# One output transfer of 128 partitions in place of four of 32

## The chip, the cores and the metric

The kernel runs on one core of one Trainium2 chip, as one program in one launch. The metric is the device time of that program in microseconds (us). The kernel before has a median of 546.88 us over three runs (542.97 to 548.76).

## What is computed

Two independent heads work on 2048 positions of width 576, and their results stand side by side in an output of 2048 rows of 1152 float32. The left half is a long convolution; the right half is a linear attention with learned feature maps.

```
# left half: the convolution
K = 2.0 * einsum("dn,dnl->dl", C, exp((A * dt)[:, :, None] * pos)).real
y = irfft(rfft(u^T, 2L) * rfft(K, 2L), 2L)[..., :L]
a = y^T + u * D_skip
# right half: linear attention, 32 heads of width 18
q, k, v = split(x @ wqkv)
phi(z) = concat([softmax(z @ w_phi), softmax(-(z @ w_phi))])
o = phi(q) (phi(k)^T v) / (phi(q) (phi(k)^T 1) + 1e-6)
b = o @ wo
out = concat([a, b], axis=-1)
```

## The kernel before, in words

The convolution is done by a Fourier transform in two factors, written as matrix products. Its inverse has two stages. `product` (L890) multiplies the spectra of the input and of the convolution's kernel for an eighth of the frequencies, does the first inverse factor, and stores the two halves of its result to scratch in DRAM (`zd`, L956). `last` (L963) does the second inverse factor. It runs 16 times: for each of two halves of the 576 columns, and in each half for eight groups of four residues `cb` to `cb + 3`. One call loads a tile `zi` of 128 rows by 4 x 288 numbers (L966, 576 KB; in the second half three of every four calls put it in a buffer named `cs`), does eight small matmuls that fill four bands of 32 PSUM partitions (one band for each residue, recorded at the helper line L295), copies the 128 x 576 result to an SBUF tile `ot` on ScalarE or VectorE (L300), and stores it (L979).

Where the tile goes sets the form of that store. Band `n` belongs to residue `n + cb`. Its 32 partitions hold 32 blocks, with two rows of 288 numbers each, so in DRAM a band is 64 pieces of 1152 bytes, 32 output rows apart. The kernel before stores each band with a transfer of its own: 32 partitions in SBUF, 64 pieces in DRAM, 72 KB.

All transfers are issued by SyncE (SP) on one queue, in an order that is written out by hand: `ORDER` is a list of operation numbers for the whole program, and each engine runs its own operations in that order, waiting in place for what the next one needs. The other operations that the prediction speaks of:

- `query_tile` of the attention ends with a matmul into PSUM, a copy into a buffer `ot`, and a store of 128 rows of 2304 bytes (L589, 288 KB). `ot` is one pool of three buffers; `last`, `query_tile` and a short step in the parameters share it, so a fourth copy waits until the store of the first has landed.
- `product` loads `ub` (L904, two transfers of 128 x 2 x 288 for each spectrum) and the matrix `ff` (L895, 256 KB).
- The transfers with narrow outer dimensions are the folds of the attention weights (L357, 126 or 72 rows), the attention state on its way through DRAM (L508 and L526 with 126 rows, L523 with 18 rows of 7 pieces) and the skip weights (L863, four pieces).

Every transfer also waits for the landing of the one eight places before it in the queue, since eight semaphores are used in turn.

Of the kernel before, what the change touches and what calls it, by code (L numbers as in the profile page):

```python
# [27 lines left out]
HD = D // 2  # L28
# [140 lines left out]
class Plan:  # L169
# [34 lines left out]
    def op(self, eng, cost, fn, r=(), w=(), with_=(), table=None, busy=1.0, lock=False, mode=(128, 128), add=None):  # L204
        deps = set()
        for b in r:
            deps.update(b.writers)
        for b in w:
            deps.update(b.readers)
        k = len(self.ops)  # L210
        eng, alt = eng if isinstance(eng, tuple) else (eng, None)
        cost, alt = cost if alt is None else cost[0], alt and (alt, cost[1])
        for b in r:
            b.readers.append(k)
        for b in w:
            b.writers.append(k)
        bufs = list({id(b): b for b in (getattr(x, "home", x) for x in (*r, *w, *with_)) if not isinstance(b, Mark)}.values())
        fill = [b for b in w if b.tag == "ps" and b.writers == [k] and not b.readers] if eng == "pe" else []
        fill = [add] if add else fill
        self.ops.append([eng, cost, fn, deps, bufs, 0.0, table, busy, lock and eng, (self.unit, 0.0, self.part), mode, fill[0] if fill else None, alt, add])  # L220
# [47 lines left out]
def c_dma(nbytes, run=4096):  # L268
    return nbytes / run * (0.35 + 0.0029 * run)
# [7 lines left out]
def body(tc, nc, i, out, ctx):  # L277
    pl = Plan()
    pe, dve, act, pool, sp = nc.tensor, nc.vector, nc.scalar, nc.gpsimd, nc.sync
# [12 lines left out]
    B, op = pl.buf, pl.op  # L292

    def mm(o, l, r, start=True, stop=True, skip=False):
        pe.matmul(o, l, r, start=start, stop=stop, skip_group_check=skip)  # L295

    def copy(eng, dst, src, r, w, n, with_=(), **kw):

        if eng == "any":
            op(("act", "dve"), (c_act(n), c_dve(n)), lambda e: act.activation(dst(), src(), AF.Copy) if e == "act" else dve.tensor_copy(  # L300
                dst(), src()), r=r, w=w, with_=with_)
        elif eng == "act":
            op("act", c_act(n), lambda: act.activation(dst(), src(), AF.Copy, **kw), r=r, w=w)
        else:
            op("dve", c_dve(n), lambda: dve.tensor_copy(dst(), src()), r=r, w=w)
# [657 lines left out]
    def last(cb, half):  # L963
        pl.at("last", 8 * half + cb // 4)
        yo, zi = B("ot", [128, 2, HD]), B("cs" if half and cb % 8 else "zi", [128, 4, HD])
        op("sp", c_dma(128 * 4608), lambda: sp.dma_start(  # L966
            zi.t, zd[half].t.rearrange("q (r b) d -> (q r) b d", r=2)[:, cb:cb + 4]), r=[zd[half]], w=[zi])
        ps = B("ps", [128, 2, HD], banks=2)
        pl.step("l1")

        def f():
            for n in range(4):
                for r in range(2):
                    mm(ps.t[32 * n:32 * n + 32, r], w3.t[64 * r:64 * r + 64], zi.t[64 * r:64 * r + 64, n])
        op("pe", 480, f, r=[zi, w3], w=[ps], mode=(64, 32))
        copy("any", lambda: yo.t, lambda: ps.t, [ps], [yo], D)
        for n in range(4):
            st = out.ap[0][0]
            op("sp", c_dma(32 * 2304, 1152), lambda n=n: sp.dma_start(bass.AP(  # L979
                tensor=out.tensor, offset=out.offset + (n + cb) * st + HD * half, ap=[[64 * st, 32], [32 * st, 2], [1, HD]]),  # L980
                yo.t[32 * n:32 * n + 32]), r=[yo])

    for half in range(2):
        for cb in range(0, 32, 4):
            last(cb, half)
# [68 lines left out]
1901 1939 1904@52 659 1900 1938 2087 770 1902@3 2038 1924 1927 1934 1937 687@57 807 771 1940@6 1925 1928 2039 772 705 660 808 1903 688 809 706 707 810  # L1054
2040@02 1930 1929 689 1941x 2200 690 691 1931@4 1932 1980 1993@64:3 2041 773x 2042 1995x 1994 1981@20 1989@64 1982x 2044 1983x 2043 774@2 708 1996 775
1990 733 709 710 711x 776 734 735 736 777 1984 778 779 1991 692@0 1985@62 1987 812@4 811 714@2 2045 715 1986x 1992 813 712@3 1988 844 713x 716@6 780
2368 2180 693 717 781 718@7 721@6 782 814 738@2 2369@4 719 694 722 720 783 784 2179 2175@0 881 2370 845 846 847 723 2183@6 2181@4 737 2389 2176 724@01
815 816 2182 725 2184 726 727 739 2185 728 817 882 883x 849@4 848 785x 850 2207 661 730@6 786@0 787 851 2372 2201 695 884 2202 2373 2250 2186 852 729
790@1 731 2187 788@0 818 819 820 2208 2375 2189 2188 2374 789 2203@4 2371 791x 732 2205@6 2390@0 2204 2243 2206 2211@4 740 2209@2 2212 2391 2190@60
2191 792@4 795@5 2307 2210 2192 821 2244 2193x 822x 823@2:6 2194 2196 2195 2242 2213x 793 2197 796 2249 2214x 2247@0 824 797 794 853 2245@6 2376@2  # L1060
2248 2246 2253@0 2347 2377 2251@4 2215@62 2198 2199 2254 2252 741 2327 885@0 2216 798@23 742 2328 799 2217 2218x 825@4 827@5 2326 800 801 826x 886
2329@6 2334 2333 828x 802 2392 2219 887 2330 2394 2382 2331@4 2332 743 2335@2 2337@6 2220 888 2336 2256 2255 2257@04 889 2258 2285 832@2 744 890 2338
2286 2259 829@3 803@4 2339x 745 2284 833 830 834 2383@6 2393 891 831 2384 2289@0 2287@2 2260 2291 892 746 2290x 835@67 893 836 894 837 2288 804 747
838 839 2261 2395 2340 2341@02 2292 2293@6 805 2295@4 748 2262 2342 2361 753@2 751@3 2343 2306 2313 2294 2296 752 754x 841@0 2305 749@3 2308@6 750
2310@4 2309x 2312 2316@2 2311 2344 2314@6 2317 2345 2381 2265 2378 755@4 2298 2297 758@5 2315 756 759 757 760 895 896x 2346 2299@26 2380 918 919 920x
761@45 762 840 806 921 2379 2270 763 2264 899@4 2300 764 2319 2348@6 2301 2318 842 2263 2266@2 900x 2267 2268@0 765 2271 2223 2388 2272@4 2349x 2303
2302x 2354 2274@6 2304 2269 955 854 2273 855 2386 856 922@2 857 2320@04 2275 923 2385 2321 2276x 901@4 897@5 956 957x 766@6 958x 898 858 767 902 2387
2229 843 2322 2222 2350 2221 2323 2228 2277 924 2362@4 2226@0 2324 2352 925 926 2224@2 2363x 2232@4 2325 2396 768 2227 927 2225 2233 2351 859 2278@60
2279 2353 2280 769 2230@2 864@4 906@5 2281 2364 2367 2355@0 2365 2366 2397@6 2282 2231 2356 2398 2234x 2283 2235x 2359 2357 2358 903@2 904 907 2236@06
905 862@3 908 909@25 865x 2237 860@4 2238 959@6 2399 960 2360 863 2239x 861x 928 866@3 910 869@4 929 930 931 911 912 2240 913 932 961 962 933 914@0  # L1070
934@2 935 938@5 2241 963 2402 870 2401 2400 939 867 964 965 966 871 868 936@6 915 916 2445 2452 937x 2446@2 2447 2417 2453@4 967 2454x 2438 943@7 917
968 969 872@60 2418@2 2431 940@1 873 874 2448 2456 2457 2449 875 876 941 944 970 971@6 975@0 878@4 972 945 2419 942 946@17 2458 947 973@6 2451 2450
877 879 976x 974x 948 2410 2455 2420 2422 2421 2423 2432@2 2439@0 2440 949 2403 2411@4 880 980@6 981 982 2424 950 2433 977@0 2444 951@2 978 2441 2436
979 983@10 2412 2442 984 2443 985 2437 986 2404@6 2435 2415 2434 2405x 2425@4 2426 2414 952 2416 2413 2409 2408 2407 2406 2428 2430 953 954 2427 2429
987 988@6 989 990 991
"""


# [16 lines left out]
```

## Time and profile before

| what | value |
|---|---|
| median of three runs | 546.88 us (542.97 to 548.76) |
| the profiled execution's own time | 545.11 us |
| its span, first to last instruction | 543.3 us |
| granted TensorE clock | 0.998 |
| TensorE busy | 521.5 us (96% of the span) |
| VectorE, ScalarE, GpSimd busy | 455.9, 382.1, 328.8 us |
| DMA engines, mean busy share of the SP queue's packets | 61.5% |
| stores of `last` (L979) | 64 issues of 72 KB, first at 421.3 us, last at 539.4 us |

Times inside the profile count from the span's start. An issue of a transfer is shown on `SPq`, with the time that SP needed for it; the data moves later, in packets on the core's 16 DMA engines. "DMA share" is the mean busy share over these 16 engines. Of the packets the page tells how many are under 512 bytes, under 2 KB and under 8 KB. "PE busy" is modelled and counts pipelined matmuls to their end.

### The profile page before, as it was taken

The numbers are of one execution on the slowest core, as the hardware profiler recorded it, in microseconds if no ns is written. First come the engines' busy times: TensorE is split into PE (matmuls) and PEld (weight loads), VectorE is DVE, ScalarE is ACT, GpSimd is POOL, SyncE is SP. The second block draws the span as 40 slices with busy tenths as digits, with TensorE's granted clock in tenths as the row PEclk, the third lists the DMA queues.
The fourth block names the chain that finished last, engine by engine and source line by source line (L and its number), as shares of the span: only waits on it lengthen the run. The fifth ranks groups of instructions, "written<-read, shape, count | busy, mean of one in ns | idle before, by whom it ended". The sixth has DMA issues, their size and how long they took to land.

```text
span 543.3 us, 19242 instructions
## 1 busy us (share of the span) xinstructions
PE 521.5 (96%) x8192; PEld 435.9 (80%) x8192; DVE 455.9 (84%) x716; ACT 382.1 (70%) x555; POOL 328.8 (61%) x456
## 2 busy tenths in 40 slices
PE   8999999999999989999999999999899999999995
PEld 7999899888888767888878666766689877776984
DVE  7999899898868889999989996999974889787641
ACT  4868798798559799889689977989733444343332
POOL 1173885958777775982758998997433617434300
PEclk9999999999999999999999999999999999999999
DMA  8936711244245678246664588756458789998785
GB/s 235 326 105 195 281 45 31 101 139 134 89 139 190 207 241 294 83 128 196 229 205 118 153 265 250 241 180 194 131 173 271 234 281 293 287 281 260 265 252 157
DMA packets 86163, 107.01 MB, mean 197 GB/s; under 512 B 5698, under 2 KB 70338, under 8 KB 86078
## 3 DMA queue, kind: packets, MB, share of 16 engines
q1 hardware_dynamic: 86078, 105.79, 61.5%
q8 instruction: 64, 1.05, 0.8%
q14 instruction: 21, 0.17, 0.1%
HBM read 61.22 MB, written 44.54 MB: 195 GB/s over the span
## 4 chain that ended last, share of the span: by engine, by line
PE 69%; DVE 13%; DMA 7%; ACT 4%; issue 3%; SPq 2%; POOL 1%; DVEq 0%; ACTq 0%; POOLq 0%
PE psum L295 63%; PE psum L549 3%; DMA ff<-in_ff_dram 2%; DMA dram<-zi 2%; PE psum L237 2%; DVE ac L314 1%; DVE cs L816 1%; SPq L979 1%; PE psum L577 1%; DMA cs<-dram 1%; DVE e L310 1%; DMA ub<-dram 1%; DVE e L314 1%; DVE small L434 1%; DVE small L437 1%
## 5 line engine op out<-in xcount | busy, mean ns | idle before, releaser
L295 PE MATMUL psum<-vh,x 128*128 128x288 f32 x576 | 123.6, 301 | 0.5 <-ACT ks L300 0.5
L295 PE MATMUL psum<-wh,x 128*128 128x288 f32 x576 | 124.1, 302 | 0.0
L757 POOL TENSOR_TENSOR cs<-cs,pi 128x32 int32<-128x32 int32 (+4 forms) x180 | 108.5, 608 | 8.0
L295 PEld LDWEIGHTS psum<-wh,x 128*128 128x128 f32 x576 | 94.1, 188 | 7.7 <-issue 4.2
L295 PEld LDWEIGHTS psum<-vh,x 128*128 128x128 f32 x576 | 94.0, 188 | 5.4 <-issue 3.2
L295 PE MATMUL psum<-vl,x 128*128 128x288 f32 x320 | 93.8, 295 | 0.0
L295 PE MATMUL psum<-wl,x 128*128 128x288 f32 x320 | 93.7, 295 | 0.0
L811 ACT ACTIVATE psum<-psum 128x512 f32<-128x512 f32 x108 | 59.9, 588 | 15.4 <-PE psum L295 14.9
L295 PEld LDWEIGHTS psum<-vl,x 128*128 128x128 f32 x320 | 60.2, 188 | 0.0
L295 PEld LDWEIGHTS psum<-wl,x 128*128 128x128 f32 x320 | 60.2, 188 | 0.0
L310 POOL TENSOR_TENSOR x<-zo,x 64x128 fp32r<-64x128 f32 (+1 forms) x30 | 25.4, 848 | 46.3 <-ACT x L394 35.1
L310 POOL TENSOR_TENSOR e<-e,small 128x1152 f32<-128x1152 f32 (+1 forms) x24 | 41.2, 1720 | 14.5 <-DVE small L450 7.8
L815 DVE TENSOR_TENSOR cs<-psum,cs 128x1024 f32<-128x1024 f32 x36 | 43.6, 1212 | 3.7 <-ACT psum L811 3.6
L310 POOL TENSOR_TENSOR e<-small,e 128x576 f32<-128x576 f32 x26 | 30.6, 1177 | 25.4 <-DVE small L437 23.6
L816 DVE TENSOR_TENSOR cs<-psum,cs 128x1024 f32<-128x1024 f32 x36 | 43.6, 1214 | 1.4 <-PE psum L295 1.3
L295 PE MATMUL psum<-ub,ff 64*32 64x288 f32 x1024 | 40.0, 410 | 4.3 <-DMA ff<-in_ff_dram 1.9
L295 PEld LDWEIGHTS psum<-kvb,fT 126*128 126x128 f32 (+1 forms) x320 | 38.3, 188 | 7.2 <-issue 2.9
L295 PEld LDWEIGHTS psum<-cs 128*32 128x32 f32 x2304 | 34.1, 110 | 11.2 <-issue 2.9
L295 PE MATMUL psum<-cs 128*32 128x64 f32 x2304 | 40.0, 220 | 2.6 <-DVE cs L816 0.9
L295 PE MATMUL psum<-kvb,fT 126*128 126x133 f32 (+1 forms) x320 | 41.6, 280 | 0.1
L440 ACT ACTIVATE e<-e 128x1152 f32<-128x1152 f32 x32 | 37.0, 1164 | 2.7 <-POOL e L310 1.3
L781 ACT ACTIVATE cs<-cs 128x1040 f32<-128x1040 int32 x36 | 38.3, 1064 | 0.6 <-POOL cs L776 0.4
(156 smaller groups left out, 1115.2 us busy)
## 6 DMA issues: line engine op xcount, KB each, us to landing
dram<-zi SPq DMA_DIRECT2D x32, 576.0 KB
ub<-dram SPq DMA_DIRECT2D x64, 288.0 KB
dram<-zo SPq DMA_DIRECT2D x32, 288.0 KB
zo<-in_xT_dram SPq DMA_DIRECT2D x24, 320.0 KB
zi<-dram SPq DMA_DIRECT2D x12, 576.0 KB
ub<-in_u_dram SPq DMA_DIRECT2D x16, 288.0 KB
xd<-x SPq DMA_DIRECT2D x8, 576.0 KB
x<-xd SPq DMA_DIRECT2D x8, 576.0 KB
```

The lines of the kernel that those rows point to most:

```text
L237: self.matmul(t[0:cols, 0:n], self.zero.t[0:rows, 0:cols], self.data.t[0:rows].bitcast(BF16)[:, 0:n], start=not o[13], stop=not o[13], ski ...
L295: pe.matmul(o, l, r, start=start, stop=stop, skip_group_check=skip)
L310: op(eng, [c_dve(n[0]) if e == "dve" else c_pool(n[1]) for e in eng], lambda e: (dve if e == "dve" else pool).tensor_tensor(dst(), a(), b( ...
L314: op(eng, c_dve(n) if eng == "dve" else c_pool(n), lambda: e.tensor_tensor(dst(), a(), b(), op=alu), r=r, w=w, with_=with_, lock=eng == "p ...
L434: op("dve", c_dve(D), lambda: dve.tensor_reduce(two(top.t), v(), axis=AX.X, op=ALU.max, negate=True), r=[p], w=[top])
L440: op("act", c_act(1152) + 40, lambda: act.activation(e.t, e.t, AF.Exp), r=[e], w=[e], table="exp")
L549: pe.transpose(tp.t[0:m, j - j0, :], e.t[:, sign, 7 * g:7 * g + GRP[g], :].rearrange("p h f -> p (h f)"), ident.t)
L757: op("pool", c_pool(2 * n * W), lambda n=n, j=j: pool.tensor_tensor(x()[:, :, :, n:2 * n], x()[:, :, :, 0:n], pi.t[:, j:j + 2, gs].bitcast ...
L781: act.activation(cs.t[:, 1], cs.t[:, 1].bitcast(I32), AF.Sin, scale=TURN)
L811: op("act", c_act(512), lambda b=b: act.activation(b.t, b.t, AF.Exp), r=[b], w=[b], table="exp")
L815: op("dve", c_dve(64 * W), lambda: dve.tensor_tensor(F(), both(M.t), F(), op=ALU.mult), r=[M, cs], w=[cs])
L816: op("dve", c_dve(64 * W), lambda: dve.tensor_tensor(E.t[:, :, :, 32:64], both(up.t), cs.t[:, :, :, 0:32], op=ALU.mult), r=[up, cs], w=[E])
```

## The change

The loop over the four bands in `last` goes. One transfer takes the whole tile of 128 partitions, and the DRAM side has one more dimension, outermost, for the four residues. The hand-written order is renumbered; the one transfer stands where the first of the four stood. The engines' compute instructions and the order of all other transfers are as before.

```
-        for n in range(4):
-            st = out.ap[0][0]
-            op("sp", c_dma(32 * 2304, 1152), lambda n=n: sp.dma_start(bass.AP(
-                tensor=out.tensor, offset=out.offset + (n + cb) * st + HD * half, ap=[[64 * st, 32], [32 * st, 2], [1, HD]]),
-                yo.t[32 * n:32 * n + 32]), r=[yo])
+        st = out.ap[0][0]
+        op("sp", c_dma(128 * 2304, 1152), lambda: sp.dma_start(bass.AP(
+            tensor=out.tensor, offset=out.offset + cb * st + HD * half, ap=[[st, 4], [64 * st, 32], [32 * st, 2], [1, HD]]), yo.t), r=[yo])
...
-2368 2180 693 717 781 718@7 721@6 782 814 738@2 2369@4 719 694 722 720 783 784 2179 2175@0 881 2370 845 846 847 723 2183@6 2181@4 737 2389 2176 724@01
+2359 2180 693 717 781 718@7 721@6 782 814 738@2 2360@4 719 694 722 720 783 784 2179 2175@0 881 2361 845 846 847 723 2183@6 2181@4 737 2371 2176 724@01
...
```

In the new kernel the store is at line L978. It writes 4 x 64 pieces of 288 numbers from 128 partitions, where the old one at L979 wrote 64 pieces from 32.

The first place is the end of SP's queue. `zi` and `cs` are the loads of `last` (L966), `out_dram<-ot` at L979 or L978 its stores, at L589 the stores of the attention. Before:

```order
L589 DMA out_dram<-ot 128x576
L966 DMA zi<-dram 128x1152
L979 DMA out_dram<-ot 64x1x288 x7
L966 DMA cs<-dram 128x1152
L979 DMA out_dram<-ot 64x1x288 x5
L966 DMA zi<-dram 128x1152
L589 DMA out_dram<-ot 128x576
L966 DMA cs<-dram 128x1152
L979 DMA out_dram<-ot 64x1x288 x18
L589 DMA out_dram<-ot 128x576
L979 DMA out_dram<-ot 64x1x288 x2
L589 DMA out_dram<-ot 128x576
```

And with the change:

```order
L589 DMA out_dram<-ot 128x576
L966 DMA zi<-dram 128x1152
L978 DMA out_dram<-ot 4x64x288 x2
L966 DMA cs<-dram 128x1152
L978 DMA out_dram<-ot 4x64x288
L966 DMA zi<-dram 128x1152
L589 DMA out_dram<-ot 128x576
L966 DMA cs<-dram 128x1152
L978 DMA out_dram<-ot 4x64x288 x5
L589 DMA out_dram<-ot 128x576 x2
```

The 32 stores of eight tiles became eight; the last quarter of the sixteenth tile, which was issued between the two last stores of the attention, now goes ahead of both.

The second place is on the same queue, some 55 us earlier, around a load of the matrix `ff` for `product`. Before:

```order
L343 DMA zo<-in_xT_dram 128x5x128
L979 DMA out_dram<-ot 64x1x288 x3
L904 DMA ub<-dram 128x2x288
L589 DMA out_dram<-ot 128x576
L904 DMA ub<-dram 128x2x288
L979 DMA out_dram<-ot 64x1x288
L895 DMA ff<-in_ff_dram 128x512
L904 DMA ub<-dram 128x2x288
```

And with the change:

```order
L343 DMA zo<-in_xT_dram 128x5x128
L904 DMA ub<-dram 128x2x288
L589 DMA out_dram<-ot 128x576
L904 DMA ub<-dram 128x2x288
L978 DMA out_dram<-ot 4x64x288
L895 DMA ff<-in_ff_dram 128x512
L904 DMA ub<-dram 128x2x288
```

Three quarters of the fourth tile are gone from the place ahead of `ub`, and ahead of `ff` stands all of the fifth tile, 288 KB, where a quarter of it stood.

## The prediction on record

> **What bounds the kernel now.** I read the busy time by stretches first, for the part in which `last` runs.
>
> ```profile
> core 0: us, PE busy (x) PEld busy (x) DVE busy (x) ACT busy (x) POOL busy (x), PEclk, DMA share, GB/s
> 440.00:490.00 50.00, 48.02 (x751) 36.94 (x750) 41.77 (x67) 21.55 (x37) 23.26 (x18) 1.00 0.94 292
> 490.00:505.00 15.00, 14.45 (x239) 10.49 (x238) 10.14 (x16) 6.74 (x11) 6.36 (x5) 1.00 0.79 254
> 505.00:514.50 9.50, 9.50 (x101) 8.70 (x100) 6.14 (x14) 3.00 (x5) 3.65 (x3) 1.00 0.78 275
> 514.50:530.00 15.50, 15.50 (x171) 13.79 (x171) 7.11 (x18) 5.71 (x11) 1.17 (x1) 1.00 0.83 251
> 530.00:543.30 13.30, 7.33 (x76) 6.00 (x74) 1.74 (x3) 2.82 (x5) 0.00 (x0) 0.93 0.52 154
> ```
>
> TensorE (PE, the first pair after the length) is busy nearly throughout, so it sets the pace. But the DMA engines stand right behind it: 94% busy from 440 to 490 us. Here a change of transfers can hurt. The end is the second view, the timeline of SP's issues and of the last matmul.
>
> ```profile
> 514.49 0.37 SPq L966 DMA_DIRECT2D zi<-dram  x1
> 514.95 5.05 SPq L979 DMA_DIRECT2D out_dram<-ot  x7
> 520.04 0.58 SPq L966 DMA_DIRECT2D cs<-dram  x1
> ...
> 525.55 12.56 SPq L979 DMA_DIRECT2D out_dram<-ot  x18
> ...
> 537.39 0.29 PE L295 MATMUL psum<-vl,x 128*128 128x288 f32 x1
> 538.21 0.53 SPq L589 DMA_DIRECT2D out_dram<-ot  x1
> 538.49 0.65 ACT L300 ACTIVATE ot<-psum 128x576 f32<-128x576 f32 x1 [2.02 <-DMA out_dram<-ot]
> ...
> 540.09 0.53 SPq L589 DMA_DIRECT2D out_dram<-ot  x1
> ```
>
> From 514.95 us SP issues stores nearly without a pause. The last matmul ends at 537.7, and the last copy still waits for an `ot` buffer, until 538.49. SP's issue time and the landing of stores thus decide about the last microsecond, while TensorE decides what stands before.
>
> **What is removed.** The line of the old stores gives the price of an issue (least, median, greatest, in ns):
>
> ```profile
> L979 SPq DMA_DIRECT2D out_dram<-ot x64: 570/589/1497, 421.3 to 539.4; - x64
> ```
>
> 48 issues of 0.589 us go: 28 us of SP's time. Most of it lies beside TensorE's work. What it can return is bounded by the waits for buffers and the tail: at least 0; at the end, a last copy right after the last matmul, 538.49 − 537.68 = 0.8 us. I keep 0.8 us for the rivals, since in my forecast something else sets the end.
>
> **On how many DMA engines the new store runs.** This is the dear question. Each transfer ends with one small completion packet on every engine it used. The quiet end shows it: from 540.7 to 543.3 us two transfers finish, the last store of each kind, and the packets under 512 bytes are 2 x 16.
>
> ```profile
> DMA packets 216, 0.36 MB, mean 138 GB/s; under 512 B 32, under 2 KB 88, under 8 KB 216
> ```
>
> The page's packet line and its narrow transfers allow a count over the whole run.
>
> ```profile
> DMA packets 86163, 107.01 MB, mean 197 GB/s; under 512 B 5698, under 2 KB 70338, under 8 KB 86078
> ...
> e<-in_wqT_dram SPq DMA_DIRECT2D x4, 315.0 KB
> ...
> e<-in_wkT_dram SPq DMA_DIRECT2D x3, 315.0 KB
> kz<-kvb SPq DMA_DIRECT2D x1, 654.6 KB
> kvb<-kz SPq DMA_DIRECT2D x1, 654.6 KB
> ...
> cs<-in_wkT_dram SPq DMA_DIRECT2D x1, 315.0 KB
> kvb<-in_wkT_dram SPq DMA_DIRECT2D x1, 180.0 KB
> e<-in_wqT_dram SPq DMA_DIRECT2D x1, 180.0 KB
> ...
> kz<-e SPq DMA_DIRECT2D x2, 46.8 KB
> ...
> dsk<-in_dsk_dram SPq DMA_DIRECT2D x4, 0.6 KB
> ```
>
> The counts of that list add up to 345 transfers. On 16 engines each they would leave 5520 completion packets; with the small pieces (2 x 126 of `kz<-e`, 4 x 4 of `dsk`) 5788 packets under 512 bytes. The page has 5698: 90 are missing. Suppose that a transfer uses the largest number up to 16 that divides its outermost dimension. Then 126 rows use 14 engines (ten transfers of 315 and 654.6 KB, 2 missing each: 20), 72 rows use 12 (two of 180 KB: 8), the 18 x 7 pieces of `kz<-e` use 9 (2 x 7 = 14), the 4 pieces of `dsk` use 4 (4 x 12 = 48). That is 90, exactly. Were it the number of pieces, `kz<-e` with 126 of them would use 14, and 80 would be missing. So the outermost dimension decides, and the new store has 4 there, on the DRAM side; 128 partitions stand on the other. No transfer of this kernel has one side below 16 and the other at 128; I take the narrower side, since a single split must suit both: 4 engines.
>
> The Trainium skill says the same of that gap (DMA: Bandwidth & Descriptors, "Why a DMA increments its semaphore by 16 and not by 1"): the count must divide the slowest dimension of both patterns. Its rules for kernel authors, on the same page, also hold a line that speaks for the change (join small transfers; one of 128 partitions for disjoint partition groups). By that line alone the store would stay on all engines, which is the first rival.
>
> **What a store on four engines costs.** 256 pieces of 1152 bytes are 64 in a row on each of four engines, where there were 16 on each of sixteen. The price of a piece comes from stretches with almost only such pieces: 498.4 to 500.1 us, dense, and 533.2 to 537.9 us, sparse. Then 508.4 to 513.9 us, only loads of `last`, and 541.2 to 541.95 us, only the last store of the attention.
>
> ```profile
> DMA packets 521, 0.55 MB, mean 325 GB/s; under 512 B 42, under 2 KB 521, under 8 KB 521
> q1 hardware_dynamic: 521, 0.55, 97.0%
> ```
>
> ```profile
> DMA packets 594, 0.54 MB, mean 115 GB/s; under 512 B 125, under 2 KB 594, under 8 KB 594
> q1 hardware_dynamic: 594, 0.54, 46.6%
> ```
>
> ```profile
> DMA packets 518, 2.17 MB, mean 394 GB/s; under 512 B 48, under 2 KB 48, under 8 KB 518
> q1 hardware_dynamic: 518, 2.17, 99.2%
> ```
>
> ```profile
> DMA packets 132, 0.27 MB, mean 366 GB/s; under 512 B 13, under 2 KB 13, under 8 KB 132
> q1 hardware_dynamic: 132, 0.27, 93.1%
> ```
>
> Share times 16 engines times length, over the pieces: 0.970 x 16 x 1.7 / 479 = 55 ns dense; 0.466 x 16 x 4.7 / 469 = 75 ns sparse; 186 ns for a piece of 4608 bytes; 94 ns for one of 2304. The new store makes a dense queue, so I take 55 ns: 64 x 55 = 3.5 us on each of the four engines, and 4.8 us at 75 ns.
>
> *The end.* From 514.49 us on, the four engines must serve eight stores of `last` (28.2 us), four loads of `last` with 8 pieces each (4 x 8 x 0.186 = 6.0 us) and three stores of the attention (3 x 8 x 0.094 = 2.3 us): 36.4 us. The last store's data begins 541.2 − 540.09 = 1.1 us after its issue, and the span ends 543.3 − 541.95 = 1.35 us after its data. So 514.49 + 1.1 + 36.4 + 1.35 = 553.4: **+10.1 us**. It is a queue without holes if tiles come fast enough: a freed `ot` buffer needs a copy (0.65), an issue (0.59) and 1.1 us until data flow, 2.3 us, while two other tiles hold the engines for 7 us. TensorE's work, done by 537.7, hides behind it. Bounds: at 75 ns +20.3. Below, the fastest stretch gives 402 GB/s, 25 GB/s an engine, 46 ns a piece:
>
> ```profile
> 528.20:530.40 2.20, 2.20 (x31) 1.90 (x30) 0.46 (x1) 0.97 (x2) 0.00 (x0) 1.00 1.05 402
> ```
>
> 8 x 64 x 46 ns = 23.6 us for the stores, +5.5 us.
>
> *Before the end.* Each of the eight earlier tiles adds (64 − 16) x 55 ns = 2.6 us to the four engines. From 440 to 490 us (four tiles) these have 6% of 50 = 3 us free and get 10.6; from 490 to 514.5 us (three tiles) they have 5.2 free and get 7.9. If nothing shrinks, that is 7.6 + 2.7 = 10.3 us late. The lower bound is 0: pieces are served faster when twelve engines are less busy, and loads have buffers in hand. The plainest place is the fifth tile, now whole in front of `ff`:
>
> ```profile
> 481.85 2.64 SPq L979 DMA_DIRECT2D out_dram<-ot  x3
> ...
> 486.18 0.58 SPq L979 DMA_DIRECT2D out_dram<-ot  x1
> 486.86 0.54 SPq L895 DMA_DIRECT2D ff<-in_ff_dram  x1
> ...
> PE psum L295 <- DMA ff<-in_ff_dram: 1.9, 3, 0.9
> ```
>
> TensorE already waits for `ff`, up to 0.9 us, so 2.6 us more in front of it shows at once, save for the 2.6 us of SP's time that the three stores at 481.85 took and now leave free. I take +2 us in all, nearer to nothing, because of these savings.
>
> **The sum.** +10.1 +2 = +12.1 us on the profiled execution's 545.11: 557.2. The median shown is 1.8 us above that execution, so I predict 559.
>
> **The rivals.**
>
> *Sixteen engines after all.* If the 128 partitions set the spread, each store costs what four did together, and SP's time is free: −0.8 us at the end. The greatest gain is what the chain of waits after 400 us gives the stores' issues:
>
> ```profile
> by line: PE psum L295 63.9%; DMA ff<-in_ff_dram 9.3%; SPq L979 4.6%; PE psum L549 4.5%; DMA cs<-dram 4.2%; PE psum L577 1.9%; DVE cs L314 1.8%; DMA out_dram<-ot 1.5%; issue 1.2%; DVE ac L314 1.0%; DVE zo L604 0.5%; ACT zo L608 0.5%; ACT ot
> ```
>
> 4.6% of 143.3 = 6.6 us. So 540 to 546, faster or no change; it decides as soon as the spread stays above about ten engines. For it: SP's crowded queue at the end. Against it: the count of 90.
>
> *Four engines, but fast.* 46 ns a piece and nothing lost earlier: +5.5, 552. For it: twelve idle engines leave room. Against: a dense queue of such pieces showed 55 ns.
>
> *The queue backs up.* Only eight transfers are under way at a time, since each waits for the eighth before it. A store that lands 5 us or more late then also holds back loads from 440 us on: 10.3 us before the end and up to 20.3 in it, near 575. For it: a DMA share of 0.94. Against: fewer transfers take the eight places.
>
> **How the numbers follow.** Forecast 0.62, sixteen engines 0.18, four but fast 0.10, backed up 0.10. A measurement here can tell about 1%, 5.5 us, from no change. Faster by more: a third of the first rival, 0.06. Within 1%: the rest of it and half of the second, 0.17. Slower: 0.77. The range leaves out most of the first rival and the top of the last: 547 to 573.
>
> **What would show it.** Packets under 512 bytes down by 48 x 16 + 16 x 12 = 960 (on sixteen engines: 768); in the last 30 us a DMA share near a quarter while the span lasts; the last copies waiting for DMA `out_dram<-ot` for 2 to 5 us each; a span near 555; `ff` waits of over 2 us. The forecast is wrong if the share at the end stays spread, or if the stores land 2 to 3 us after their issue.

## The result and the profile after

The changed kernel takes 564.86 us (median of six runs, 562.71 to 567.95); the kernel before, on the same chips, 545.48 us (six runs, 542.97 to 548.92). The ratio is 1.035, with a 95% interval of 1.030 to 1.041: 19.4 us slower. The range held the time. The step before the end did not hold, as will be seen.

First the packet line of the page after, which answers the question of the engines.

```profile
DMA packets 85203, 107.01 MB, mean 190 GB/s; under 512 B 4738, under 2 KB 69378, under 8 KB 85118
```

5698 − 4738 = 960 small packets fewer, the number that four engines for each store give. The data packets are the same: all 1152-byte pieces are still there, on fewer engines. Next, the transfers from 551.5 to 556 us, when only pieces of the stores of `last` moved: packets by size, then the queue's packets, MB and share of 16 engines. Below them stand the last two copies into `ot`, which waited until a store of `last` had landed; the one before them, at 552.82 us, had waited 5.58 us.

```profile
DMA packets 372, 0.42 MB, mean 93 GB/s; under 512 B 8, under 2 KB 372, under 8 KB 372
...
q1 hardware_dynamic: 372, 0.42, 27.2%
```

```profile
555.99 0.65 ACT L300 ACTIVATE ot<-psum 128x576 f32<-128x576 f32 x1 [2.52 <-DMA out_dram<-ot]
...
559.15 0.65 ACT L300 ACTIVATE ot<-psum 128x576 f32<-128x576 f32 x1 [2.51 <-DMA out_dram<-ot]
```

A share of 27% is 4.35 of 16 engines. At least two stores were under way all through that stretch (issued at 543.7, 545.8, 550.4 and 553.5 us; the three copies show the first three of them landed by 552.8, 556.0 and 559.1), and yet not eight engines worked: each store takes the same four. 364 pieces kept them busy for 0.272 x 16 x 4.5 = 19.6 us, 54 ns a piece. The estimate was 55. That is a time of packets, and such times overlap a little, since four engines have only 18 us in 4.5. The pace was 4 x 4.5 us / 364 = 49.5 ns a piece, 3.2 us a store, which is also the distance of the landings.

Busy time by stretches, as shown of the kernel before (the last row is the part that it did not have):

```profile
core 0: us, PE busy (x) PEld busy (x) DVE busy (x) ACT busy (x) POOL busy (x), PEclk, DMA share, GB/s
440.00:490.00 50.00, 45.01 (x696) 32.31 (x702) 36.69 (x59) 19.37 (x33) 21.66 (x16) 0.97 0.86 263
490.00:505.00 15.00, 12.95 (x192) 8.86 (x181) 9.21 (x13) 4.46 (x8) 5.14 (x5) 0.89 0.79 250
505.00:514.50 9.50, 9.48 (x128) 7.92 (x121) 7.45 (x13) 4.54 (x8) 2.73 (x2) 1.00 0.42 127
514.50:530.00 15.50, 12.29 (x112) 11.07 (x110) 7.70 (x17) 3.22 (x5) 4.71 (x4) 0.91 0.66 228
530.00:543.30 13.30, 13.30 (x138) 11.07 (x137) 4.61 (x12) 4.43 (x9) 0.07 (x1) 0.85 0.66 224
543.30:564.50 21.20, 10.24 (x98) 8.86 (x96) 2.67 (x6) 3.87 (x7) 0.00 (x0) 0.85 0.33 120
```

TensorE had holes of 5 us from 440 to 490 us, 2 us from 490 to 505 and 3 us from 514.5 to 530, where it had 2, 0.5 and none. The mean DMA share fell although the bytes are the same and four engines had more to do. It misleads as soon as the work is not spread. SP's issues show where the program stood still. Before, around the hand-over from the first column half to the second:

```profile
502.51 1.16 SPq L956 DMA_DIRECT2D dram<-zo  x2
...
506.54 0.47 SPq L966 DMA_DIRECT2D zi<-dram  x1
```

And after:

```profile
506.21 1.87 SPq L956 DMA_DIRECT2D dram<-zo  x2
508.17 1.24 SPq L978 DMA_DIRECT2D out_dram<-ot  x2
511.93 1.73 SPq L956 DMA_DIRECT2D dram<-zo  x2
521.32 0.33 SPq L966 DMA_DIRECT2D zi<-dram  x1
...
541.63 12.41 SPq L978 DMA_DIRECT2D out_dram<-ot  x5
```

The first load of the second half (L966 at 521.32) stood at 506.54 before: 14.8 us late. It needs the whole intermediate result in DRAM, whose last store was issued at 512.7 us. Before, that store was issued at 503.31 us, so 9.4 us of the delay had already gathered ahead of it; the wait for its landing added the other 5.4. The chain of waits gives that store 8.41 us to land, and the last store of `last` but one 8.63 us:

```profile
512.72 8.41 DMA dram<-zo
...
550.42 8.63 DMA out_dram<-ot
```

And the waits for transfers over the whole run (total, times, longest), before:

```profile
ACT ot L300 <- DMA out_dram<-ot: 8.5, 5, 2.7
...
ACT x L394 <- DMA zo<-in_xT_dram: 7.3, 4, 3.5
```

And after:

```profile
ACT ot L300 <- DMA out_dram<-ot: 13.2, 5, 5.6
ACT x L394 <- DMA zo<-in_xT_dram: 12.4, 5, 7.0
...
ACT zo L608 <- DMA dram<-zo: 6.9, 2, 3.9
...
DVE zo L604 <- DMA dram<-zo: 3.7, 1, 3.7
```

The copies at the end wait for the stores, as forecast. But `ff`, named as the plainest place, is waited for by nobody any more. What came late were loads of the attention's input and the landing of the intermediate result's stores; both move through the `zo` buffers, and a buffer is free only when its store has landed.

### The profile page after: what moved, and what is told of

Its sections match the earlier page's. It is cut to its first block, busy times and chain, and to the rows that moved or that the text cites. A ratio compares the mean times of both kernels' runs of the same rounds, so it can differ in the third digit from the quotient of the medians.

```text
span 564.5 us, 19176 instructions
## 1 busy us (share of the span) xinstructions
PE 530.4 (94%) x8192; PEld 440.6 (78%) x8192; DVE 457.1 (81%) x716; ACT 382.0 (68%) x555; POOL 328.4 (58%) x456
## 2 busy tenths in 40 slices
DMA packets 85203, 107.01 MB, mean 190 GB/s; under 512 B 4738, under 2 KB 69378, under 8 KB 85118
## 4 chain that ended last, share of the span: by engine, by line
PE 56%; DMA 16%; DVE 12%; POOL 7%; ACT 4%; issue 3%; SPq 1%; DVEq 0%; ACTq 0%; POOLq 0%
PE psum L295 53%; DMA dram<-zo 4%; DMA zo<-in_xT_dram 2%; PE psum L549 2%; DMA ub<-dram 2%; POOL cs L757 2%; DMA out_dram<-ot 2%; POOL ac L310 1%; DMA kz<-kvb 1%; DMA e<-in_wkT_dram 1%; DVE zo L604 1%; DVE e L310 1%; POOL cs L776 1%; DMA cs<-dram 1%; DVE cs L314 1%
## 5 line engine op out<-in xcount | busy, mean ns | idle before, releaser
L295 PE MATMUL psum<-ub,ff 64*32 64x288 f32 x1024 | 42.3, 428 | 4.5 <-issue 2.1
L295 PEld LDWEIGHTS psum<-kvb,fT 126*128 126x128 f32 (+1 forms) x320 | 40.4, 197 | 7.7 <-issue 3.4
L295 PE MATMUL psum<-kvb,fT 126*128 126x133 f32 (+1 forms) x320 | 43.7, 289 | 0.1
L314 DVE TENSOR_TENSOR ac<-ac,psum 128x1152 f32<-128x1152 f32 x24 | 31.7, 1347 | 9.7 <-PE psum L295 5.9
```

What stands on the lines that cost most here:

```text
L314: op(eng, c_dve(n) if eng == "dve" else c_pool(n), lambda: e.tensor_tensor(dst(), a(), b(), op=alu), r=r, w=w, with_=with_, lock=eng == "p ...
```

## The experiments

**One store for each tile, its outermost dimension 16, 8, 4 or 2.** Four kernels differ from the changed one by the DRAM pattern alone; in them the rows go to other places of the output, so that the pattern can be cut as wished. SBUF side, bytes, pieces and places in the order are the same.

```
-            tensor=out.tensor, offset=out.offset + cb * st + HD * half, ap=[[st, 4], [64 * st, 32], [32 * st, 2], [1, HD]]), yo.t), r=[yo])
+            tensor=out.tensor, offset=out.offset + cb // 4 * st + HD * half, ap=[[8 * st, M], [16 * M * st, 128 // M], [8 * M * st, 2], [1, HD]]), yo.t), r=[yo])
# M = 16, 8, 4 or 2
```

For 16:

> One store per tile as in the changed kernel, same bytes and pieces, but the DRAM pattern's outermost dimension is 16 (the rows are written to other places of the output, so the left half is not the reference's). Theory (the outermost dimension sets the number of engines): 16 engines, 16 pieces of 1152 bytes on each, as with four stores; stores land 3 to 4 us after their issue; the time is that of the kernel before less up to 0.8 us at the end, 544 to 547 us. Rival (joining the four stores costs, since a tile's buffer is free only when all 288 KB have landed): 560 to 568 us, as the changed kernel.

For 8:

> As d16 with an outermost dimension of 8. Theory: 8 engines, 32 pieces each, 1.8 us a store at 55 ns a piece. At the end 8 x 1.8 + 8.2 = 22 us of work fit into the 28 us there, so the end is not bound by it; before it each store adds 0.9 us to eight engines, which hides for the most part: 546 to 551 us. Rival (joining): 560 to 568 us.

For 4:

> As d16 with an outermost dimension of 4, that is the changed kernel with other output rows. Theory: 4 engines, the time of the changed kernel within 1%, 560 to 570 us, stores landing 7 to 10 us after their issue. Rival (it is the rows' places in DRAM, one row apart on four engines at the same time, that slow the stores): here the engines write rows eight apart, and the time differs from the changed kernel's by over 1%.

For 2:

> As d16 with an outermost dimension of 2. Theory: 2 engines, 128 pieces each, 7.0 us a store. At the end 8 x 7.0 + 8.2 = 64 us where 28 stood, +38 us; before the end 8 x (128 - 16) x 55 ns = 49 us more on two engines with some 14 us free there, +35 us: about 620 us, 595 to 640. Rival (joining): 560 to 568 us.

Measured beside a median of 545.01 us for the kernel before:

| outermost dimension | time, us | ratio, 95% interval |
|---|---|---|
| 16 | 542.13 (ten runs) | 0.9945, 0.992 to 0.997 |
| 8 | 544.21 (ten runs) | 1.0005, 0.998 to 1.003 |
| 4 | 566.46 (one run) | |
| 2 | 606.02 (one run) | |

The ratios are those on record and not quotients of the medians shown.

The packet lines, in that order:

```profile
DMA packets 85395, 107.01 MB, mean 197 GB/s; under 512 B 4930, under 2 KB 69570, under 8 KB 85310
```

```profile
DMA packets 85267, 107.01 MB, mean 197 GB/s; under 512 B 4802, under 2 KB 69442, under 8 KB 85182
```

```profile
DMA packets 85204, 107.01 MB, mean 190 GB/s; under 512 B 4739, under 2 KB 69379, under 8 KB 85119
```

```profile
DMA packets 85171, 107.01 MB, mean 177 GB/s; under 512 B 4706, under 2 KB 69346, under 8 KB 85086
```

Without any packet of these stores 5698 − 64 x 16 = 4674 would be left. The rest is 256, 128, 65 and 32: sixteen stores times 16, 8, 4 and 2 engines (one packet over in the third, which also has one more instruction packet, 22 in place of 21). With 2, the stretch from 585 to 592 us has the share of 2.2 engines at 47 GB/s:

```profile
DMA packets 285, 0.33 MB, mean 47 GB/s; under 512 B 2, under 2 KB 285, under 8 KB 285
...
q1 hardware_dynamic: 285, 0.33, 13.5%
```

That is 2 x 7 us / 283 = 49.5 ns a piece again.

So the DRAM side's outermost dimension sets the number of engines though 128 partitions stand on the other side, which the profile of before could not show. Joining the stores costs nothing: the kernel with 16 engines is even 0.55% faster than the kernel before. Its rows stand in other places, though, so the gain is not shown to be the joining's alone. The rows' places do not explain the loss, as the kernel with 4 takes the changed kernel's time in its one run. With 8, the extra work is hidden. The kernels with 16 and 8 came out below the ranges expected of them, those with 4 and 2 inside.

**Each half alone.** The one store on four engines only for the tiles of the first column half, all issued before the hand-over to the second, or only for those of the second.

```
+        if not half:     # "half" in the other kernel: one store
...
+        else:            # four stores, as before
+            for n in range(4):
```

The first half:

> Only the tiles of the first column half (the first eight calls) use the one store on four engines; the last eight keep four stores each. Theory from the trace of the changed kernel: its loads for the second half are issued 14.8 us later than before (506.5 to 521.3) and the next ones 11.6 us later (514.5 to 526.1), so most of the loss arises before the end: +9 to +12 us here, 554 to 557 us. The prediction's own split gave +2 before the end: 547 us.

The second:

> Only the tiles of the second column half use the one store on four engines. Theory: the end is a queue on four engines of eight stores, four loads and three attention stores, +8 to +11 us, 553 to 556 us. If the loss before the end alone sets the time (the rival: the late loads are what counts, and the end would have been hidden without them): 545 to 548 us.

Beside 544.95 us: the first half alone 558.12 us (ratio 1.023, 1.020 to 1.027), +13.2 us; the second alone 554.08 us (1.016, 1.014 to 1.019), +9.1 us. Both are near what the trace of the changed kernel gave, though the first lies 1 us above its range, and together they are 3 us more than the two at once cost. The prediction's +2 for the first half is refuted. In the kernel of the first half, the hand-over has the holes of the changed kernel (the first load at 520.51 us), and no end on few engines:

```profile
514.50:530.00 15.50, 12.07 (x114) 10.34 (x120) 6.92 (x15) 3.75 (x6) 4.79 (x4) 0.90 0.66 229
530.00:556.90 26.90, 21.20 (x232) 18.28 (x216) 7.28 (x17) 7.78 (x15) 0.00 (x0) 0.94 0.67 196
```

In the kernel of the second half the first load is issued at 505.17 us (506.54 before), and the end runs at a share of 0.30. TensorE's hole of 3.4 us from 514.5 to 530 us is a wait for a load `cs` that was issued behind two of the stores, so it belongs to the end (`cs` takes every second tile of the second half, not three of every four):

```profile
514.50:530.00 15.50, 12.09 (x134) 10.15 (x133) 4.74 (x14) 4.18 (x8) 1.17 (x1) 0.93 0.67 212
530.00:551.60 21.60, 11.28 (x103) 10.03 (x101) 2.84 (x6) 4.12 (x7) 0.00 (x0) 0.82 0.30 107
```

**Is it the line on one queue, or the engines' time?** Other transfers could be late because they stand behind 64 pieces on each of four engines, which a second queue or another order would mend; or because those engines have no time left. First, the stores on ScalarE's queue, at the same places of the order:

```
-        op("sp", c_dma(128 * 2304, 1152), lambda: sp.dma_start(bass.AP(
+        op("act", c_dma(128 * 2304, 1152), lambda: act.dma_start(bass.AP(
```

> All as in the changed kernel, but ScalarE issues the sixteen stores, on its own queue, at the same places of the order. They still run on four engines. Theory (other transfers of the one queue wait in line behind 64 pieces on each of the four engines): with a second queue their packets alternate with the store's, so the stores of the intermediate result land sooner, the loads for the second half are issued 5 to 12 us sooner than in the changed kernel, and the end is bound by the four engines as before: 551 to 559 us. Rival (the four engines have no time left, whatever the order): 561 to 568 us.

574.69 us (ratio 1.055, 1.051 to 1.058): worse than either theory had it. On this queue the stores stand alone, with 4160 packets: 16 x (256 + 4), four completion packets for each. The loads for the second half came no sooner, at 520.49 us against 521.32:

```profile
520.49 0.33 SPq L966 DMA_DIRECT2D zi<-dram  x1
520.87 0.42 SPq L966 DMA_DIRECT2D cs<-dram  x1
```

That speaks for the rival at the hand-over. The profiled execution is 6 us longer than that of the changed kernel (spans of 570.6 and 564.5 us), and all of it comes after these loads; the rest of the 10 us between the medians the trace does not show. A new standstill is part of it. ScalarE's own copy into `ot` waited 6.36 us until a store had landed, and the two next stores stood behind this copy in ScalarE's order:

```profile
536.98 0.55 ACTq L978 DMA_DIRECT2D out_dram<-ot  x1
...
547.40 0.65 ACT L300 ACTIVATE ot<-psum 128x576 f32<-128x576 f32 x1 [6.36 <-DMA out_dram<-ot]
547.46 1.21 ACTq L978 DMA_DIRECT2D out_dram<-ot  x2
```

Meanwhile the DMA engines ran dry (share 0.09, the next to last figure):

```profile
545.00:548.00 3.00, 0.00 (x0) 0.00 (x0) 0.00 (x0) 0.60 (x1) 0.00 (x0) 0.93 0.09 35
```

Then the order. Two operation numbers of the hand-written order, the stores issued at 508.2 and 508.8 us, were moved back behind the last two stores of the intermediate result. On SP's queue, before and after that edit:

```
978 out<-ot, 956 x2, 978 out<-ot x2, 956 x2, 966 x4, 589, 966, 978 x2, ...
978 out<-ot, 956 x4, 966 x4, 589, 966, 978 x4, ...
```

> The changed kernel with two of its stores (the two issued at 508.2 and 508.8 us, in front of the last two stores of the intermediate result) moved on SP's queue behind these, the first loads of the second half and one attention store. In the changed kernel SP waits until 521.3 us for the intermediate result, whose stores stand behind those two. Theory A (a chain: what the two stores delay is this hand-over, and the twelve other engines stand still meanwhile): the loads are issued 5 to 7 us sooner and the kernel gains most of that, 558 to 562 us. Theory B (the four engines are busy without a hole from 440 us to the end, so their total work sets the time and no order of the stores helps): 563 to 568 us, as the changed kernel, the loads issued sooner all the same.

567.10 us (ratio 1.040, 1.038 to 1.043), where the changed kernel has 564.86 (ratio 1.035, 1.030 to 1.041): theory B. The loads were issued 8.6 us sooner, and the time came back in the store that followed:

```profile
512.74 0.33 SPq L966 DMA_DIRECT2D zi<-dram  x1
...
521.28 0.37 SPq L966 DMA_DIRECT2D zi<-dram  x1
521.69 9.48 SPq L978 DMA_DIRECT2D out_dram<-ot  x4
```

TensorE was busy for 3.16 of the 8 us from 522 on:

```profile
522.00:530.00 8.00, 3.16 (x36) 2.26 (x35) 0.15 (x1) 1.41 (x3) 0.00 (x0) 0.94 0.49 152
```

**Is SP's issue time worth something?** The kernel before, with two of the four stores of each tile of the second half issued by ScalarE:

```
+            q = "act" if half and n % 2 else "sp"
-            op("sp", c_dma(32 * 2304, 1152), lambda n=n: sp.dma_start(bass.AP(
+            op(q, c_dma(32 * 2304, 1152), lambda n=n, q=q: (act if q == "act" else sp).dma_start(bass.AP(
```

> The kernel before with its four stores on sixteen engines; in the second half ScalarE issues two of the four. It takes 16 issues of 0.59 us from the crowded end of the queue. If the run with 16 engines and one store each was 0.55% faster because of the issue time saved, this one gains up to the same: 542 to 544 us. If ScalarE's own work waits behind the issues: 545 to 548 us.

546.16 us (ratio 1.001, 0.999 to 1.004): no difference. The 0.55% of the kernel with one store on 16 engines is not to be had in this way, and why its gain is 3 us and not the 0.8 us expected stays open. That kernel is the fastest measured here, but its rows stand in the wrong places; the four residues of a tile are its outermost dimension in the true output, and I have no correct pattern that starts with 16.

## Why the prediction was right, and which step was off

*The engines.* "So the outermost dimension decides": shown, by the completion packets of four sizes and by shares of 27% and 13.5%. The count of before, 90 missing packets, was enough to find it before any run. The Trainium skill's rule (DMA: Bandwidth & Descriptors, "Rules for kernel authors", on using all 16 engines) states it in the same sense: an outermost dimension under 16 confines the whole transfer to at most that many engines. The runs agree, at 8, 4 and 2. The Trainium skill's line on joining small transfers, in the same section, is borne out only where the spread stays whole, by the 0.55% of the kernel with 16.

*The price of a piece.* 55 ns forecast, 54 ns measured, both as times of packets. The sum for the end needs the pace, though, and that was 49.5 ns, inside the bounds of 46 and 75: 25.3 us for eight stores where the forecast had 28.2.

*The end.* +10.1 us forecast; the second half alone shows +9.1. In the changed kernel, the same stretch from the fifth load of the second half on (514.49 before, 526.11 after) to the span's end grew from 28.8 to 38.4 us: +9.6. With the pace just given, the forecast's own sum would have been +7.3, so the closeness is in part luck; what made up the other 2 us the runs do not single out.

*Before the end.* Forecast: "I take +2 us in all, nearer to nothing, because of these savings", between bounds of 0 and 10.3. Measured: +13.2 us alone, and 526.11 − 514.49 = 11.6 us in the changed kernel. This is the term that was mis-sized, and beyond its upper bound; that the total still fell into the range is owed to the width of the range. The upper bound, the added work less the free time, was near; the choice of +2 far below it was not. SP's saved issue time was set against engine time, yet the run that only moved issues off SP gained nothing. And the engines' free time was taken for usable in each stretch, while part of it stands where nothing may be issued: at the hand-over SP waits for the intermediate result to land. The latter was not tested by itself.

One count over the whole stretch, made here after the fact, gives about the size. Before, from 440 to 543.3 us, an engine was busy for 86.0 us (0.94 x 50 + 0.79 x 15 + 0.78 x 9.5 + 0.83 x 15.5 + 0.52 x 13.3). Fifteen tiles add 15 x 48 x 55 ns = 39.6 us to four of them: 125.6 us from 440 on, a span of 565.6. The span after is 564.5. The same count for the time after: the shares of its table give 84.8 engine-us each; without the stores' own 13.0 (15 x 256 x 54 ns over 16) and with 51.8 for the four (15 x 64 x 54 ns) it is 123.6 of 124.5 us. By this count the four engines had hardly any time to spare, and the two kernels that change the queue or the order but not this work did not get faster. For 8 engines the count is 86.0 + 13.2 (15 x 16 x 55 ns) = 99.2, within the 103.3 us that the stretch has: no loss, as measured. For 2 it is 178.4, a span of 618; measured 604.3. With the pace of 49.5 ns for the stores the count gives spans of 560 for 4 engines and 608 for 2, so it is good to about 4 us.

It does not say that the four engines never stood still. At the hand-over of the changed kernel the share is 0.04, less than one engine of 16:

```profile
520.00:522.00 2.00, 2.00 (x18) 2.00 (x17) 0.69 (x1) 1.75 (x3) 0.06 (x1) 1.00 0.04 11
```

How much of the 11.6 us is work of the four engines and how much is waiting at the hand-over is not separated; that a better order alone does not win the time back is shown for the one order tried.

*The signs.* The 960 packets came as said. The last three copies waited 5.6, 2.5 and 2.5 us for `ot`, about the 2 to 5 us that were named. The share near a quarter came only from 545 to 557 us (0.27); over the last 30 us it was 0.42. The `ff` waits did not come, and the span was 564.5 instead of near 555.

## What to carry to other kernels

Before joining transfers, look at the outermost dimension of both patterns: an outermost 4 put the whole transfer on four engines here, with 128 partitions on the other side, and the count of small packets, less the small pieces of data, shows how many engines a kernel's transfers really use. Then count the work of the fullest engines from the first such transfer to the end, all transfers that pass them included; a mean share tells nothing of them, and time saved on the issuing queue does not pay for theirs. Moving a store to the queue of an engine that also fills its buffers can leave the DMA engines empty, since the engine waits in its own order.

## What the runs showed of the hardware that was not expected

The granted TensorE clock fell together with TensorE's busy share, in the profiled executions: a mean of 0.998 before (96% busy), 0.976 after (94%) and 0.948 with two engines (89%). The kernel with two engines shows it most in its last stretch, with TensorE busy less than half of the time at a granted clock of 0.69:

```profile
530.00:604.30 74.30, 34.93 (x297) 28.36 (x295) 9.93 (x22) 11.54 (x20) 2.64 (x3) 0.69 0.33 115
```

Whether it costs time of its own was not tried. The issue of a store on four engines (0.564 us in the median, at L978) took SP no longer than one of a quarter of its size on sixteen (0.589 us).
